# A fused linear-attention and GLU kernel: a shorter warm-up of TensorE, the up weights on another queue, and new orders of all engines

## The chip, the cores and the metric

The kernel runs on one core of one Trainium2 chip. The core has five engines with a queue of instructions each, strictly in order: TensorE (PE in the profile; its weight loads are shown apart as PEld), VectorE (DVE), ScalarE (ACT), GpSimd (POOL) and SyncE (SP, which here only starts DMAs). PE multiplies a stationary tile of weights with a moving tile and writes to PSUM, which has eight banks here; VectorE and ScalarE read PSUM and write SBUF. DMAs started from SP and from ACT stand in two queues, q1 and q10 in the profile. The metric is the time of one execution on the device in microseconds (us); less is better.

## The reference

One transformer block on 2048 rows of 448 columns in bf16: a linear attention with 16 heads of 28 columns, then a gated feed-forward part of width 1792, each with a layer norm ahead and a residual addition behind.

```python
def _A_ref(x, wqkv, wo):
    ...
    phi = lambda t: jnp.where(t > 0, t + 1, jnp.exp(t)) + 1e-6
    pq, pk = phi(q), phi(k)
    kv = jnp.einsum("bhsd,bhse->bhde", pk, v)
    z = jnp.einsum("bhsd->bhd", pk)
    num = jnp.einsum("bhqd,bhde->bhqe", pq, kv)
    den = jnp.einsum("bhqd,bhd->bhq", pq, z)[..., None] + 1e-6
    o = num / den
    ...
def _B_ref(x, w_gate, w_up, w_down):
    ...
    h = _gelu(g) * u
    ...
h = x + _A_ref(_layernorm(x, axis=-1), A_wqkv, A_wo)
h2 = h + _B_ref(_layernorm(h, axis=-1), B_w_gate, B_w_up, B_w_down)
```

## The kernel before

The rows are cut into 16 tiles of 128 (t = 0 to 15). The work has four stages that run into each other.

**Norm and K.** For each tile VectorE takes the statistics (`ln_stats`, L438 and L439), ScalarE turns the variance into rs by a logarithm and an exponential (L445, L447), and the normalized tile xnn is written by VectorE for tiles 0 to 2 (L478) and by GpSimd for the others (L481; from tile 4 on L505, and L508 for the last 64 columns of odd tiles). The PE transposes tiles 0 to 3 (L493), whose results ScalarE (L500) and VectorE (L502) copy into xnT, a part of the tensor hh; from tile 4 on SP starts DMA transposes instead (L512), for single tiles 4 to 7 and for pairs from 8 on. Then PE multiplies with the K weights (`proj1` L534 for tiles 0 and 1, `proj2` L553 for pairs). ScalarE takes the exponential e (L570), VectorE clips it (L571) and makes pk of it (L573), and PE sums the products of pk with the normalized rows over all tiles (`pt_pair`, L588). A group of L553 cannot write its banks before pk of the group that used them is done.

**Q and the small matrices.** The Q products (L553 as well) go to eq and pq (L596, L597). The sums of L588 are copied out, multiplied with the V weights (L629, kv), masked (L633) and multiplied with the output weights (L645, w2).

**Attention output.** For each pair of tiles the denominators are formed by a product with z (L680, GpSimd), a sum (L684) and a reciprocal (L687); pq is scaled (L689, L694), transposed (by PE for the first pair, by DMA L717 later), multiplied with w2 (L734, L749), added to x (L756), and normalized again into hn and its transpose hnT.

**Feed-forward.** `gu_chunk` multiplies gate and up weights with hnT (L872, L874), ScalarE takes the gelu (L896), VectorE the product hm (L898), and PE multiplies with the down weights (L823, L841). The first chunks of 2 tiles stand between the attention output of later pairs.

**What sets the order.** `_Graph.add` records each task with the buffers that it reads and writes. The numbers in ORDERS are those tasks, one string of them per engine: PE, ACT, DVE, POOL, SP. `place` puts them in that order and `plan` works out the semaphore waits that are left. HOLD sets which of several waits of a task comes first. So each engine's queue is written out by hand, and a task that waits holds all behind it.

**Around the change.** The first task of PE is the warm-up `warm_fn` (L422 to L427): WARM matmuls of ones_bf with itself into a bank that nobody reads, as soon as GpSimd has written the ones. The transposes of tile 0 follow, then the task `fill_0`, eight matmuls of the same kind (L433), then K of tile 0. The loads of x and of the Q and K weights are listed in LOADS (L255): SP starts x of tile 0, the K and Q weights and x of tiles 4 to 15, ACT starts x of tiles 1 to 3. The gate and up weights (L614, L615; 1568 KB each, gate to partitions 0 to 63 and up to 64 to 127) are started by SP behind the last DMA transpose of x; behind them in SP's queue stand the copies of w2 (L663) and the transposes of L717. Two memsets of VectorE (L411 on wv_sb, L412 on pt_sb) and some of GpSimd (L397 eps_d, L404 a part of xnn, L410 pqn) and its two selects (L406, L408) prepare buffers and stand wherever ORDERS puts them.

## Time and profile before

| what | before |
|---|---|
| median of 3 runs | 193.06 us (192.75 to 193.07) |
| the profiled execution | 193.89 us |
| its span in the trace | 191.7 us |
| instructions in the trace | 4775, of them 2030 matmuls |
| bytes moved | 17.59 MB |

The profile is one further execution with the hardware profiler on. Its span runs from the first to the last instruction; 2.2 us lie around it. A row of the timeline has the start and the length in us, the engine, the source line, the operation, the tensor written and those read, shapes and count; in square brackets stands the idle time of the engine ahead of it and what ended it. In the rows by stretch, each engine has its busy time and the number of its instructions in the stretch; the last three columns are the recorded clock, the busy share of the DMA engines and GB/s. Matmuls are pipelined: the time of one in a row is longer than the distance to the next. Rows that end in KB and a number are DMA issues: size, and the time from issue to landing.

### The profile page before, as it was taken

Reading aid. Unit: us, or ns where it says so; the run is one execution under the profiler, and the core shown is the slowest. Engines: PE = TensorE matmul, PEld = TensorE weight load, DVE = VectorE, ACT = ScalarE, POOL = GpSimd, SP = SyncE. Lnnn points to the kernel's source line nnn. Section 1 sums busy time; section 2 is a strip of 40 time slices with the busy share of each in tenths; the row PEclk is TensorE's granted clock in tenths of the full one; section 3 lists DMA queues with packets and bytes.
Section 4 is the critical chain, followed back from the end, with each engine's and each line's share of the span. In section 5 each row is a group of like instructions: output and inputs, shape, how many; then the busy total and the mean of one; then the engine's idle time right before and its main releaser. Section 6 shows DMA issues by size and latency. Waiting matters only on the chain.

```text
span 191.7 us, 4775 instructions
## 1 busy us (share of the span) xinstructions
PE 185.4 (97%) x2030; PEld 104.1 (54%) x2030; DVE 124.7 (65%) x260; ACT 71.7 (37%) x164; POOL 53.9 (28%) x102
## 2 busy tenths in 40 slices
PE   7999989999799999999999999999999999999994
PEld 7735545554498758774444444444555444454443
DVE  2699957799999989996858773416444153434222
ACT  3498433678874202322222322121444032442100
POOL 3079930075056538641019003510000000000000
DMA  6924579997649543392050650007400002000004
GB/s 180 336 72 100 115 166 248 208 215 161 98 117 226 140 77 81 72 148 55 13 99 5 144 96 3 0 0 108 87 0 3 0 3 96 0 3 0 0 27 168
DMA packets 34244, 17.59 MB, mean 92 GB/s; under 512 B 27312, under 2 KB 32944, under 8 KB 34224
## 3 DMA queue, kind: packets, MB, share of 16 engines
q1 hardware_dynamic: 33936, 16.95, 40.2%
q8 instruction: 16, 0.26, 0.6%
q10 hardware_dynamic: 288, 0.34, 0.5%
q14 instruction: 4, 0.03, 0.1%
HBM read 8.37 MB, written 1.84 MB: 53 GB/s over the span
## 4 chain that ended last, share of the span: by engine, by line
PE 84%; DVE 4%; POOL 4%; ACT 3%; DMA 2%; issue 1%; POOLq 0%
PE ps L872 42%; PE ps L823 19%; PE ps L553 5%; PE ps L749 5%; PE ps L588 4%; PE ps L425 3%; PE ps L841 3%; DMA hh<-xnn 2%; PE ps L874 2%; POOL xnn L505 2%; DVE st L438 1%; ACT pq L597 1%; POOL xnn L508 1%; ACT ln L445 1%; DVE x_sb L756 1%
## 5 line engine op out<-in xcount | busy, mean ns | idle before, releaser
L872 PE MATMUL ps<-hnT,wgu_sb 64*128 64x512 bf16 (+1 forms) x490 | 88.4, 333 | 0.1
L874 PE MATMUL ps<-hnT,wgu_sb 64*128 64x512 bf16 (+1 forms) x490 | 88.4, 333 | 0.0
L896 ACT ACTIVATE gl<-ps 128x256 bf16<-128x256 f32 (+1 forms) x84 | 34.9, 453 | 87.3 <-PE ps L872 87.3
L898 DVE TENSOR_TENSOR hh<-ps,gl 128x256 bf16<-128x256 f32 (+1 forms) x84 | 40.2, 507 | 40.8 <-ACT gl L896 40.7
L872 PEld LDWEIGHTS ps<-hnT,wgu_sb 64*128 64x128 bf16 x490 | 46.0, 94 | 35.3 <-ACT gl L896 0.5
L874 PEld LDWEIGHTS ps<-hnT,wgu_sb 64*128 64x128 bf16 x490 | 45.9, 94 | 0.5
L823 PE MATMUL ps<-wd_sb,hh 64*128 64x448 bf16 x392 | 39.4, 349 | 0.0
L823 PEld LDWEIGHTS ps<-wd_sb,hh 64*128 64x128 bf16 x392 | 18.9, 94 | 18.6 <-issue 0.4
L680 POOL TENSOR_TENSOR t<-pq,zbc 128x448 f32<-128x448 bf16 x15 | 16.7, 1128 | 30.4 <-DVE zbc L617 12.6
L553 PE MATMUL ps<-wqk_sb,hh 64*128 64x448 bf16 x196 | 23.4, 350 | 1.3 <-DMA hh<-xnn 0.7
L438 DVE BATCH_NORM_STATS2 st<-x_sb 128x6 f32<-128x448 bf16 x32 | 19.0, 609 | 3.5 <-DMA x_sb<-in_A_x_dram 3.4
L588 PE MATMUL ps<-pk,xnn 64*128 64x448 bf16 x128 | 15.5, 349 | 0.4 <-DVE pk L573 0.4
L553 PEld LDWEIGHTS ps<-wqk_sb,hh 64*128 64x128 bf16 x196 | 9.3, 95 | 10.9 <-DMA hh<-xnn 1.1
L828 DVE TENSOR_TENSOR x_sb<-ps,x_sb 128x896 bf16<-128x896 f32 x7 | 7.6, 1090 | 6.5 <-PE ps L823 6.5
L570 ACT ACTIVATE e<-ps 128x896 bf16<-128x896 f32 (+1 forms) x10 | 7.6, 766 | 7.8 <-PE ps L553 7.7
L772 POOL TENSOR_SCALAR hn<-x_sb,nm,rs 128x448 bf16<-128x448 bf16 x14 | 10.1, 727 | 0.5
L749 PE MATMUL ps<-w2p,pqnT 64*128 64x448 bf16 x84 | 9.9, 349 | 0.0
L588 PEld LDWEIGHTS ps<-pk,xnn 64*128 64x128 bf16 x128 | 6.5, 94 | 6.3 <-DVE pk L573 1.1
L756 DVE TENSOR_TENSOR x_sb<-ps,x_sb 128x896 bf16<-128x896 f32 (+1 forms) x9 | 8.7, 973 | 0.6 <-PE ps L749 0.6
L573 DVE SCALAR_TENSOR_TENSOR pk<-ps,e 128x896 bf16<-128x896 f32 (+1 forms) x10 | 8.8, 893 | 0.1
L684 DVE TENSOR_REDUCE den<-t 128x32 f32<-128x896 f32 (+1 forms) x9 | 8.7, 969 | 0.2 <-POOL t L680 0.2
L505 POOL TENSOR_SCALAR xnn<-x_sb,nm,rs 128x448 bf16<-128x448 bf16 (+1 forms) x12 | 8.3, 696 | 0.9 <-ACT rs L447 0.9
(85 smaller groups left out, 141.8 us busy)
## 6 DMA issues: line engine op xcount, KB each, us to landing
wgu_sb<-in_B_w_gate_dram SPq DMA_DIRECT2D x1, 1568.0 KB, 11.4
wgu_sb<-in_B_w_up_dram SPq DMA_DIRECT2D x1, 1568.0 KB, 18.5
out_dram<-x_sb SPq DMA_DIRECT2D x7, 224.0 KB, 2.2
x_sb<-in_A_x_dram SPq DMA_DIRECT2D x3, 448.0 KB, 6.4
wd_sb<-in_B_w_down_dram SPq DMA_DIRECT2D x2, 448.0 KB, 3.9
wqk_sb<-in_A_wqkv_dram SPq DMA_DIRECT2D x2, 336.0 KB, 4.7
wd_sb<-in_B_w_down_dram SPq DMA_DIRECT2D x2, 336.0 KB, 4.1
wo_sb<-in_A_wo_dram SPq DMA_DIRECT2D x1, 392.0 KB, 4.6
```

Source lines behind the costliest of these rows:

```text
L438: op("dve", lambda e: e.bn_stats(st[:, t, :], src_ap), [b_src], [b_st[t]], "bnst%s_%d" % (tag, t))
L505: op("pool", lambda e: e.tensor_scalar(xnn[:, p, o:o + w1], x_sb[:, t, 0:w1], nm1[:, t:t + 1], rs1[:, t:t + 1], ALU.add, ALU.mult), [b_x[t ...
L553: ins = e.matmul(ps[:, bk0 + i_, 0:D], xnT[HALF[h], t, c, :], wqk_sb[HALF[h], c, c0:c0 + D], start=(part == "a" and c == 0), stop=(c == 3))
L588: ins = e.matmul(ps[:, BK_PT[c], 0:D], xnn[HALF[h], t // 2, tcols(t, c)], pk[HALF[h], t % PK_R, :], start=(t == 0 and o == 0), stop=(t == ...
L680: op(eng, lambda e, t=t, n=n: e.tensor_tensor(t1[:, n, :], pq[:, t, :], zbc[:, :], ALU.mult), [b_pq[t]] + b_z, [b_t1[n]], "t1%s_%d" % (eng ...
L749: ins = e.matmul(ps[:, BK_OUT[n], 0:D], pqnT[rows, i2, n, g, :], w[rows, g, :], start=(g == 0 and s == 0), stop=(g == 3 and s == 1))
L756: op("dve", lambda e, t=t, bo=bo, m=m: e.tensor_tensor(x_sb[:, t:t + m, :], ps[:, bo:bo + m, 0:D], x_sb[:, t:t + m, :], ALU.add), b_ps[bo: ...
L823: ins = e.matmul(ps[:, BK_O[n], 0:D], hh[HALF[h], j, (t % HR) * 128:(t % HR + 1) * 128], wd_sb[HALF[h], j, :], start=(s == 0 and j == 0), ...
L872: first = e.matmul(psG[:, jj * N:(jj + 1) * N], wgu_sb[A_, k, j * 128:(j + 1) * 128], hnT[A_, r0:r0 + nt, ka_, :], start=(k == 0), stop=(k ...
L874: ins = e.matmul(psU[:, jj * N:(jj + 1) * N], wgu_sb[B_, k, j * 128:(j + 1) * 128], hnT[B_, r0:r0 + nt, kb_, :], start=(k == 0), stop=(k = ...
L896: G.add("act", lambda e, gi=gi, cs_=cs_, psG=psG: e.activation(gl[:, gi, cs_], psG[:, cs_], AF.Gelu_apprx_tanh), r=[b_ps[BK_G[i]]], w=b_gl ...
L898: op("dve", lambda e, dst=dst, srcU=srcU, srcL=srcL: e.tensor_tensor(dst, srcU, srcL, ALU.mult), [b_ps[bu]] + b_glh, [b_ar[j_][t % HR] for ...
```

## The change

WARM becomes 58, and each warm-up matmul writes 64 columns where it wrote 128. The eight of the fill stay as they are. The up weights are started by ScalarE's queue and not by SyncE's. ORDERS and HOLD are new for all five engines. The line of WARM_N is added, so each line behind it has a number one higher in the changed kernel.

```diff
 ORDERS = (
...
-    "1 3 26 30 31 38 39 34 46 47 62 54 42 55 66 67 50 98 99 59 69 105 106 81 122 82 123 85 129 130 148 149 94 95 168"
...
+    "1 3 26 30 31 38 34 39 46 47 62 42 54 55 67 50 66 98 99 59 69 105 106 122 82 81 123 85 129 130 148 149 95 94 168"
...
-    WARM = 56
+    WARM = 58
+    WARM_N = 64
...
         def warm_fn(e):
             ins = None
             for _ in range(WARM):
-                ins = e.matmul(ps[:, 3, 0:128], ones_bf[:], ones_bf[:], start=True, stop=True)
+                ins = e.matmul(ps[:, 3, 0:WARM_N], ones_bf[:], ones_bf[:, 0:WARM_N], start=True, stop=True)
             return ins
...
         dma("sp", wgu_sb[A_, :, :], B_w_gate.rearrange("(k p) n -> p k n", p=64), b_wg, "dwg0", behind=xts[-1:])
-        dma("sp", wgu_sb[B_, :, :], B_w_up.rearrange("(k p) n -> p k n", p=64), b_wu, "dwu0", behind=xts[-1:])
+        dma("act", wgu_sb[B_, :, :], B_w_up.rearrange("(k p) n -> p k n", p=64), b_wu, "dwu0", behind=xts[-1:])
```

`dma` turns `behind` into a place in the same queue if the transpose was started by the same engine, and into a wait for its landing if not. So ScalarE now waits for the last DMA transpose of x, at a place between the exponential of tiles 12 and 13 and those of tiles 15 and 14; SyncE's queue has the copies of w2 right behind gate.

The orders at three places. First the start of VectorE's queue. BN_STATS and BN_AGGR are the statistics of a tile, TENSOR_SCALAR on xnn is a normalization (the first that of tile 0), and COPY takes the transposes of a tile out of PSUM. Before:

```order
L438 BN_STATS st1<-x_sb 128x6
L439 BN_AGGR mv1<-st1 128x2
L438 BN_STATS st1<-x_sb 128x6
L411 MEMSET wv_sb 64x224
L478 TENSOR_SCALAR xnn<-x_sb,mv1,rs1 128x448
L439 BN_AGGR mv1<-st1 128x2
L438 BN_STATS st1<-x_sb 128x6
L502 COPY hh<-ps 128x4x64
```

After:

```order
L439 BN_STATS st1<-x_sb 128x6
L440 BN_AGGR mv1<-st1 128x2
L439 BN_STATS st1<-x_sb 128x6
L479 TENSOR_SCALAR xnn<-x_sb,mv1,rs1 128x448
L440 BN_AGGR mv1<-st1 128x2
L439 BN_STATS st1<-x_sb 128x6
L503 COPY hh<-ps 128x4x64
```

The memset of wv_sb has left the place ahead of the first normalization.

Second, VectorE around the clip and pk of tiles 4 and 5 and, further on, of tiles 12 and 13. The 128x896 rows on e1 are clips of a pair, SCALAR_TENSOR_TENSOR is pk of a pair, and the rows on eq and pq prepare Q. Before:

```order
L438 BN_STATS st1<-x_sb 128x6 x2
L439 BN_AGGR mv1<-st1 128x2 x2
L571 TENSOR_SCALAR e1<-e1 128x896
L573 SCALAR_TENSOR_TENSOR pk<-ps,e1 128x896
...
L571 TENSOR_SCALAR e1<-e1 128x896
L573 SCALAR_TENSOR_TENSOR pk<-ps,e1 128x896
L571 TENSOR_SCALAR e1<-e1 128x448 x2
```

After:

```order
L439 BN_STATS st1<-x_sb 128x6 x3
L440 BN_AGGR mv1<-st1 128x2 x2
L572 TENSOR_SCALAR e1<-e1 128x896
L574 SCALAR_TENSOR_TENSOR pk<-ps,e1 128x896
...
L572 TENSOR_SCALAR e1<-e1 128x896
L412 MEMSET wv_sb 64x224
L574 SCALAR_TENSOR_TENSOR pk<-ps,e1 128x896
```

Three statistics in a row, not two, stand ahead of the clip of tiles 4 and 5, and the memset of wv_sb now stands between clip and pk of tiles 12 and 13.

Third, GpSimd from tile 7 to the pair of tiles 10 and 11, whose DMA transpose starts when both are normalized. The rows on nm1 negate means, the rows of 128x448, 128x384 and 128x64 on xnn are normalizations. Before:

```order
L505 TENSOR_SCALAR xnn<-x_sb,nm1,rs1 128x384
L508 TENSOR_SCALAR xnn<-x_sb,nm1,rs1 128x64
L442 TENSOR_SCALAR nm1<-mv1 128x2
L508 TENSOR_SCALAR xnn<-x_sb,nm1,rs1 128x64
L505 TENSOR_SCALAR xnn<-x_sb,nm1,rs1 128x448
L408 AFFINE_SELECT mask<-mtmp 112x4
L505 TENSOR_SCALAR xnn<-x_sb,nm1,rs1 128x384
L442 TENSOR_SCALAR nm1<-mv1 128x2
L508 TENSOR_SCALAR xnn<-x_sb,nm1,rs1 128x64
L505 TENSOR_SCALAR xnn<-x_sb,nm1,rs1 128x384
L397 MEMSET eps_d 128x1
L442 TENSOR_SCALAR nm1<-mv1 128x2
```

After:

```order
L443 TENSOR_SCALAR nm1<-mv1 128x2
L398 MEMSET eps_d 128x1
L509 TENSOR_SCALAR xnn<-x_sb,nm1,rs1 128x64
L506 TENSOR_SCALAR xnn<-x_sb,nm1,rs1 128x384
L509 TENSOR_SCALAR xnn<-x_sb,nm1,rs1 128x64
L506 TENSOR_SCALAR xnn<-x_sb,nm1,rs1 128x448
L443 TENSOR_SCALAR nm1<-mv1 128x2
L411 MEMSET pqn 128x16x16
L506 TENSOR_SCALAR xnn<-x_sb,nm1,rs1 128x448
L509 TENSOR_SCALAR xnn<-x_sb,nm1,rs1 128x64
L405 MEMSET xnn 128x6x64
L506 TENSOR_SCALAR xnn<-x_sb,nm1,rs1 128x384
```

The memsets of pqn and of a part of xnn, which stood ahead of tile 4, now stand between the normalizations of tiles 10 and 11, and the select L408 has moved behind the last normalization.

On PE the groups of L588 change places with the K products of later tiles (pt of tiles 2 and 3 stands one group later), the w2 products stand together ahead of Q of tiles 10 and 11, both parts of the output product of tiles 4 and 5 stand together, and most gate and up groups run in rising order where before each second pair was swapped.

72 rows, old and new, of tables (HOLD, ORDERS) are left out of this document.

## The prediction

> **What bounds the kernel now.** I read the page first, then the busy time by stage, then the timeline of TensorE (PE) where a stage shows idle time, and last the timelines of the engine that PE waits for there.
>
> The page, its span and the busy time of each engine:
>
> ```profile
> span 191.7 us, 4775 instructions
> PE 185.4 (97%) x2030; PEld 104.1 (54%) x2030; DVE 124.7 (65%) x260; ACT 71.7 (37%) x164; POOL 53.9 (28%) x102
> ```
>
> PE is the bound, but a share of the span doesn't say where it waits. Busy time by stage, columns as the heading of the view has them (stretch, its length, busy time of each engine):
>
> ```profile
> 25.65:40.20 14.55, 14.55 (x153) 7.30 (x153) 10.75 (x20) 6.73 (x11) 1.99 (x3) 1.00 0.97 218
> 40.20:61.70 21.50, 20.28 (x293) 14.17 (x292) 20.23 (x41) 16.55 (x30) 9.86 (x12) 1.00 0.74 151
> 61.70:190.00 128.30, 127.49 (x1352) 68.13 (x1352) 74.12 (x148) 32.78 (x83) 25.84 (x46) 1.00 0.26 53
> ```
>
> From 61.70 us on PE is busy 127.49 of 128.30 us, and the change leaves it the same 1352 matmuls. So nothing can be won there; the new orders can only lose. From 25.65 to 40.20 PE has no idle time at all: when that stretch starts sets when the rest ends. What can be won lies ahead of 25.65, and up to 1.2 us between 40.20 and 61.70. PE's timeline ahead of 25.65 (start, length, line, count, idle time before it):
>
> ```profile
> 1.05 5.95 PE L425 MATMUL ps<-ones_bf 128*128 128x128 bf16 x56 [1.05 <-POOL eps_t L396]
> 6.93 0.29 PE L493 MATMUL ps<-ident,xnn 64*128 64x64 bf16 x8
> 7.15 0.62 PE L433 MATMUL ps<-ones_bf 128*128 128x128 bf16 x8
> 7.70 1.03 PE L534 MATMUL ps<-wqk_sb,hh 128*128 128x448 bf16 x4
> 8.78 1.03 PE L534 MATMUL ps<-wqk_sb,hh 128*128 128x448 bf16 x4
> 12.42 0.72 PE L553 MATMUL ps<-wqk_sb,hh 64*128 64x448 bf16 x5 [0.43 <-ACT hh L500]
> 21.60 0.93 PE L588 MATMUL ps<-pk,xnn 64*128 64x448 bf16 x8 [0.41 <-DVE pk L573]
> 25.65 0.74 PE L553 MATMUL ps<-wqk_sb,hh 64*128 64x448 bf16 x6 [0.66 <-DMA hh<-xnn]
> ```
>
> The 56 warm-up matmuls hold the transposes of tile 0 (L493) until 6.93. After them PE waits three times: for an evacuation on ScalarE (0.43), for pk on VectorE (0.41), and for a DMA transpose (0.66).
>
> **The warm-up.** Its pace is the only place where the trace shows PE's clock, since the clock column says 1.00 throughout. Matmuls of L425 by stretch:
>
> ```profile
> 1.00:3.20 2.20, 2.15 (x21) 2.15 (x22) 1.00 0.60 124
> 3.20:6.60 3.40, 3.40 (x35) 3.40 (x34) 1.00 1.11 337
> 6.92 0.17 PEld L493 LDWEIGHTS ps<-ident,xnn 64*128 64x128 bf16 x8
> ```
>
> The 56 take 5.95 us, one per 0.106, and up to 6.60 the stretches keep that pace (35 are in flight in 3.40 us, some three of them begun before). The eight fills of L433 right after take 0.62 us in all, under 0.08 each with the last one's drain. So PE runs at half pace until about 6.6 us and at full pace from there. At half pace 64 columns should take half of 0.106; the weight loads are no hindrance, since eight loads of 128 columns took 0.17 us at full pace (0.021 each, 0.04 at half pace). Estimate: 58 x 0.053 = 3.1 us, and the warm-up ends at 4.15 instead of 7.00.
>
> Who then comes last? VectorE and ScalarE ahead of tile 0, and the loads (size, us from issue to landing):
>
> ```profile
> 4.60 0.20 ACT L447 ACTIVATE rs<-ln 128x1 f32<-128x1 f32 x1
> 4.86 0.24 DVE L411 MEMSET wv_sb<- 64x224 uint32 x1
> 5.13 0.40 DVE L478 TENSOR_SCALAR xnn<-x_sb,mv,rs 128x448 bf16<-128x448 bf16 x1
> 1.25 1.02 SPq L359 DMA_DIRECT2D wqk_sb<-in_A_wqkv_dram  x2
> wqk_sb<-in_A_wqkv_dram SPq DMA_DIRECT2D x1, 112.0 KB, 4.4
> 3.48 0.58 SPq L359 DMA_DIRECT2D x_sb<-in_A_x_dram  x1
> x_sb<-in_A_x_dram SPq DMA_DIRECT2D x1, 448.0 KB, 5.9
> ```
>
> The memset of wv_sb leaves its place ahead of tile 0's normalization (L478), which then starts at 4.84 behind rs (4.80) and ends at 5.24, not 5.53. Transposes start at about 5.3, the fills follow (eight at half pace, 0.86 us, to 6.35), and the K weights land at 1.7 + 4.4 = 6.1. K of tile 0 starts at about 6.4 instead of 7.70: 1.3 us earlier, if PE runs at full pace.
>
> Here I have to choose. Before, PE was busy without a break for 5.5 us (1.05 to 6.6) when the pace doubled. Now it is busy for 3.1, idle for 1.1 and busy again from 5.3. I take it that the break starts the count anew, so that the pace doubles by 5.3 + 5.5 = 10.8 at the latest, and reckon with 10.4. [...]
>
> At half pace the four matmuls of 448 columns take 4 x 0.374 = 1.5 us and eight transposes some 0.3, so a step from one projection to the next is 1.8 instead of the 1.08 between 7.70 and 8.78. K of tile 1 starts at 6.4 + 2 x 1.8 = 10.0, and before it was 7.70 + 2 x 1.08 = 9.87. So the lead of 1.3 us is gone by then. What is left: ScalarE and VectorE have done more of tiles 0 and 1 by then, the second memset (L412, same kind) no longer sits ahead of the first pk, and the row at 12.42, which waited for ScalarE, comes at about 12.1: **-0.3** (between -0.7, half the lead, and +0.2).
>
> **Pair by pair to 25.65.** VectorE around the wait at 21.60, then the piece of the chain of work that ended last from 21.20 on, and the times to landing of the transposes of x:
>
> ```profile
> 18.44 0.61 DVE L438 BATCH_NORM_STATS2 st<-x_sb 128x6 f32<-128x448 bf16 x1
> 19.67 0.75 DVE L571 TENSOR_SCALAR e<-e 128x896 bf16<-128x896 bf16 x1 [0.34 <-ACT e L570]
> 20.45 1.09 DVE L573 SCALAR_TENSOR_TENSOR pk<-ps,e 128x896 bf16<-128x896 f32 x1
> 21.20 4.40 DMA hh<-xnn
> DMA to landing us min/median/max: 2.4/2.8/4.4
> ```
>
> Three statistics now stand ahead of this e (L571), not two: 0.61 less the 0.34 of idle time is +0.27 on pk, so of the 0.3 only **-0.03** is left at 21.60. PE was done at 24.99 (25.65 less 0.66) and would now be at 24.96. The transpose of tiles 10 and 11 ended 4.40 us after GpSimd was done at 21.20, against a median of 2.8. GpSimd:
>
> ```profile
> 12.10 0.71 POOL L505 TENSOR_SCALAR xnn<-x_sb,nm,rs 128x448 bf16<-128x448 bf16 x1 [0.36 <-ACT rs L447]
> 10.62 0.31 POOL L410 MEMSET pqn<- 128x256 bf16 x1
> 10.87 0.42 POOL L404 MEMSET xnn<- 128x384 bf16 x1
> 18.02 0.19 POOL L408 TENSOR_SCALAR_AFFINE_SELECT mask<-mtmp 112x4 f32<-112x4 f32 x1
> q8 instruction: 1, 0.02, 5.0%
> ```
>
> Two memsets (0.73 us) move from idle time into the dense run between tile 4 and tile 11, one select (0.19) leaves it: 21.2 - 12.1 = 9.1 becomes 9.2 to 9.6, since up to 0.4 of waits in it can absorb some. With tile 4 at 11.8 (0.3 earlier, as its transposes on PE are) the last is done at about 21.1, and the transpose lands at 23.9 (median) or 25.5 (as slow as before). A 16 KB instruction load ran between 23.2 and 24.6 (last row), beside the slow one's end; it follows PE's progress, which hardly moves against the transpose, so neither case can be left out. K of tiles 10 and 11 starts at 24.96 or at 25.5: -0.69 or -0.15, and I take the middle, **-0.42**.
>
> **Later.** The memset of wv_sb now stands between an e and its pk (tiles 12 and 13), the pk that Q of tiles 4 and 5 waits for:
>
> ```profile
> 31.79 1.09 DVE L573 SCALAR_TENSOR_TENSOR pk<-ps,e 128x896 bf16<-128x896 f32 x1
> 33.04 0.73 PE L553 MATMUL ps<-wqk_sb,hh 64*128 64x448 bf16 x6
> ```
>
> pk ended at 32.88, PE started at 33.04 without a wait and could not have by 0.1 us more: 0.24 of memset and 0.1 of gaps less 0.1 is **+0.24** (0 to +0.35).
>
> The up weights on ScalarE's queue, the gate and up rows of the same view:
>
> ```profile
> wgu_sb<-in_B_w_gate_dram SPq DMA_DIRECT2D x1, 1568.0 KB, 11.4
> wgu_sb<-in_B_w_up_dram SPq DMA_DIRECT2D x1, 1568.0 KB, 18.5
> 29.06 0.62 SPq L359 DMA_DIRECT2D wgu_sb<-in_B_w_up_dram  x1
> 32.87 0.98 ACT L570 ACTIVATE e<-ps 128x448 bf16<-128x448 f32 x2 [1.54 <-PE ps L553]
> 52.49 0.27 PE L872 MATMUL ps<-hnT,wgu_sb 64*128 64x256 bf16 x1
> ```
>
> They landed at 29.1 + 18.5 = 47.6, and their first use is at 52.49, so 4.9 us of cover remain whether they come sooner or, beside gate, as late as now. The issue, some 0.6 us on ScalarE, waits there for the last transpose of x with the e of tiles 14 and 15 queued behind; that e idled 1.54 us for a product of the same transpose. Zero, and +0.3 if that transpose lands late.
>
> From 40.20 to 61.70 the regrouped w2, Q and output products fill waits that sit beside a latency chain of VectorE and ScalarE, which stays: **-0.07** for the small ones that go (-0.3 to +0.5; the upper end is the product hm of L898 ahead of the first down projection, behind two copies and an addition now).
>
> **Sum:** -0.42 + 0.24 - 0.07 = -0.25 us (the -0.3 and -0.03 are contained in -0.42). The profiled execution took 193.89 us, 2.2 of it outside its span; it would take 193.64. The median of the runs shown is 193.06, 0.83 below the profiled one, and the difference carries over: 192.8.
>
> **Rivals.** *The pace doubles at about 6.65 all the same.* Then the lead of 1.3 us is kept, 1.4 with the memset; tile 4 is bound by its load, 3.48 + 5.9 = 9.4, which leaves GpSimd about 1.4 as well. At 21.60 -1.13 is left. PE is done at 23.86, the transpose lands at 22.9 to 24.5: K of tiles 10 and 11 at 23.86 to 24.5, -1.79 to -1.15, middle -1.47; with the later terms -1.3, so 191.8. For it: 1.1 us of idle time is short. Against: 5.5 busy microseconds were needed before.
>
> *The pace comes later still,* because the projections at half pace leave small gaps and the count starts only with the closer work from about 8 us on: 8.0 + 5.5 = 13.5. K of tile 1, the transposes of tile 3 and Q of tile 1 run at half pace too; the row at 12.42 comes at about 13.4, +1.0, and that at 21.60 at +1.2. PE is done at 26.2, after any transpose: +0.5; with +0.24 and -0.07 it is +0.7, so 193.8. It decides from a doubling at about 11.3 us on; before that the idle time at 25.65 absorbs it. For it: the gaps of the projections are in the rows of before (a step of 1.08 us holds four matmuls of 0.2 and eight transposes). Against: the break of 1.1 us is far longer than those.
>
> *The small matmuls are no shorter,* because each loads 128 columns of weights, and the warm-up ends near 7 as now. Then only the moved statistics, memsets and selects count: GpSimd is done near 21.4, PE is done at 25.26 (+0.27), the transpose lands at 24.2 to 25.8: -0.39 to +0.15, with the later terms about zero, 193.1. The row of the weight loads speaks against it. [...]
>
> **How the numbers follow.** Forecast 0.48, early pace 0.28, late pace 0.16, no shorter 0.08. About 0.2%, 0.39 us, is what a measurement of this kernel can tell from no change. The forecast's own range is 192.3 to 193.4; its middle lies inside no change but near its edge, so it gives 0.18 to faster, 0.25 to same, 0.05 to slower. Early pace is faster but for 0.01 of same; late pace gives 0.11 to slower and 0.05 to same; the last gives 0.06 to same and 0.01 to each side. Together 0.46, 0.37, 0.17. The range, 191.5 to 193.6, leaves out some 0.18: the lower third of early pace and over half of late pace.
>
> **What would show it.** L425's rows, now L426: 58 in about 3.1 us. The first K row near 6.4, with a step to the next of 1.8 (forecast), 1.1 (early pace). The row at 12.42 near 12.1, that at 25.65 between 24.9 and 25.5, Q at 33.04 with a wait for pk of about 0.2. The prediction is wrong if the first step is 1.1, or if PE shows idle time past 61.7, where the new order would have cost what the front won.

## The result and the profile after

| what | before | after |
|---|---|---|
| median of the runs of the comparison | 193.06 us (192.75 to 193.81, 4 runs) | 195.92 us (193.56 to 196.18, 4 runs) |
| ratio, 95% interval | | 1.012 (1.0074 to 1.0166) |
| profiled execution, its span | 193.89 us, 191.7 us | 196.02 us, 194.3 us |
| timed again on a second chip, 12 runs | 193.34 | 193.80 (192.40 to 195.44), ratio 1.0024 (0.9996 to 1.0053) |
| timed again on a third chip, 12 runs | 192.84 | 194.48 (192.75 to 196.19), ratio 1.0057 (1.0035 to 1.0080) |

The change makes the kernel slower, in two of the three comparisons by more than the noise, and it spreads its times: over the three comparisons its 28 runs go from 192.40 to 196.19, while 127 runs of the kernel before in the later comparisons lie between 192.46 and 194.41. Seven of the 28 have a mean clock of 0.99; before has 0.999 or more in all. A ratio leaves out runs over 1.5% above the fastest of their kernel, most of which have the lower clock, so the medians, which are over all runs, say more here.

The page of the changed kernel: its span, the busy time of PE, and the two rows of 40 slices for PE and its clock.

```profile
span 194.3 us, 4777 instructions
PE 186.6 (96%) x2032; PEld 102.5 (53%) x2032; DVE 124.9 (64%) x260; ACT 71.7 (37%) x164; POOL 53.8 (28%) x102
PE   6999959999989999999999999999999999999995
PEclk9999978999999999999999999999999999999999
```

A slice is 4.86 us: PE is idle for almost half of the sixth (from 24.3 us), and its clock is lower in the sixth and the seventh. PE's timeline, first the front, then from 21 us on:

```profile
1.05 3.27 PE L426 MATMUL ps<-ones_bf 128*128 128x64 bf16 x58 [1.05 <-POOL eps_t L397]
5.29 0.40 PE L494 MATMUL ps<-ident,xnn 64*128 64x64 bf16 x8 [0.97 <-DVE xnn L479]
6.52 1.76 PE L535 MATMUL ps<-wqk_sb,hh 128*128 128x448 bf16 x4
8.43 1.67 PE L535 MATMUL ps<-wqk_sb,hh 128*128 128x448 bf16 x4
10.15 1.03 PE L535 MATMUL ps<-wqk_sb,hh 128*128 128x448 bf16 x4
...
21.14 0.93 PE L589 MATMUL ps<-pk,xnn 64*128 64x448 bf16 x8
23.61 0.92 PE L589 MATMUL ps<-pk,xnn 64*128 64x448 bf16 x8
26.52 0.94 PE L554 MATMUL ps<-wqk_sb,hh 64*128 64x448 bf16 x6 [2.00 <-DMA hh<-xnn]
28.01 1.70 PE L554 MATMUL ps<-wqk_sb,hh 64*128 64x448 bf16 x8
29.50 1.71 PE L589 MATMUL ps<-pk,xnn 64*128 64x448 bf16 x12
31.05 0.73 PE L554 MATMUL ps<-wqk_sb,hh 64*128 64x448 bf16 x6
```

The front is close to the forecast: a warm-up of 3.27 us with its last matmul's end, K of tile 0 at half pace at 6.52, K of tile 1 at 10.15 at full pace. The row of 21.60 is now at 21.14 and waits for nothing. Then K of tiles 10 and 11 starts at 26.52 instead of 25.65, behind 2.00 us of idle time, and from 27 to 30.3 us the groups take twice as long. The row that stood at 28.50 stands at 31.05: +2.55 us, where the spans differ by 2.6. Its row in the kernel before:

```profile
28.50 0.73 PE L553 MATMUL ps<-wqk_sb,hh 64*128 64x448 bf16 x6
```

The chain of work that ended last has the transpose it waits for as one piece of 5.23 us (4.40 before), and the DMA queues in the middle of it, from 23.0 to 24.6 us, hold two loads of instructions (q8 is the 16 KB block of the prediction's last GpSimd row):

```profile
21.24 5.23 DMA hh<-xnn
...
q8 instruction: 1, 0.02, 5.6%
q14 instruction: 1, 0.01, 5.5%
```

The trace's record of TensorE's clock changes at 9.86, 26.93 and 30.34 us; the distances are 17.07 and 3.41, that is 5 and 1 times 3.413. Busy time by stretch, cut at those edges:

```profile
20.11:23.52 3.41, 3.41 (x38) 1.67 (x36) 3.04 (x6) 1.44 (x4) 3.31 (x8) 1.00 0.67 138
23.52:26.93 3.41, 1.42 (x18) 0.52 (x14) 2.19 (x4) 0.92 (x1) 2.12 (x5) 1.00 0.90 91
26.93:30.34 3.41, 3.41 (x22) 1.39 (x20) 0.00 (x0) 0.59 (x1) 0.00 (x0) 0.50 1.05 256
64.50:192.60 128.10, 127.50 (x1352) 68.31 (x1352) 74.51 (x148) 33.11 (x83) 26.27 (x46) 1.00 0.26 53
```

In the stretch in which PE waits it is busy for 1.42 of 3.41 us, and for the whole next stretch its clock is 0.50: 22 matmuls where 38 to 40 fit, some 1.7 us. From 64.5 us on nothing is lost.

### The profile page after: what moved, and what is told of

The parts are those of the page before. It is cut to its first block, busy times and chain, and to the rows that moved or that the text cites. A ratio compares the mean times of both kernels' runs of the same rounds, so it can differ in the third digit from the quotient of the medians.

```text
span 194.3 us, 4777 instructions
## 1 busy us (share of the span) xinstructions
PE 186.6 (96%) x2032; PEld 102.5 (53%) x2032; DVE 124.9 (64%) x260; ACT 71.7 (37%) x164; POOL 53.8 (28%) x102
## 4 chain that ended last, share of the span: by engine, by line
PE 81%; DMA 6%; DVE 5%; POOL 4%; ACT 3%; issue 1%; POOLq 0%
PE ps L873 42%; PE ps L824 19%; PE ps L750 5%; PE ps L554 4%; PE ps L589 3%; PE ps L842 3%; DMA hh<-xnn 3%; DMA pqnT<-pqn 2%; POOL xnn L506 2%; PE ps L875 2%; PE ps L535 1%; DMA x_sb<-in_A_x_dram 1%; DVE pqn L690 1%; POOL xnn L509 1%; ACT e L571 1%
## 5 line engine op out<-in xcount | busy, mean ns | idle before, releaser
L554 PE MATMUL ps<-wqk_sb,hh 64*128 64x448 bf16 x196 | 24.5, 362 | 2.2 <-DMA hh<-xnn 2.0
L681 POOL TENSOR_TENSOR t<-pq,zbc 128x448 f32<-128x448 bf16 x15 | 17.6, 1182 | 31.5 <-DVE zbc L618 15.4
L589 PE MATMUL ps<-pk,xnn 64*128 64x448 bf16 x128 | 16.5, 364 | 0.0
L554 PEld LDWEIGHTS ps<-wqk_sb,hh 64*128 64x128 bf16 x196 | 9.4, 96 | 12.7 <-DMA hh<-xnn 2.4
## 6 DMA issues: line engine op xcount, KB each, us to landing
wgu_sb<-in_B_w_gate_dram SPq DMA_DIRECT2D x1, 1568.0 KB, 12.3
```

The source lines that it names most:

```text
L554: ins = e.matmul(ps[:, bk0 + i_, 0:D], xnT[HALF[h], t, c, :], wqk_sb[HALF[h], c, c0:c0 + D], start=(part == "a" and c == 0), stop=(c == 3))
L589: ins = e.matmul(ps[:, BK_PT[c], 0:D], xnn[HALF[h], t // 2, tcols(t, c)], pk[HALF[h], t % PK_R, :], start=(t == 0 and o == 0), stop=(t == ...
L681: op(eng, lambda e, t=t, n=n: e.tensor_tensor(t1[:, n, :], pq[:, t, :], zbc[:, :], ALU.mult), [b_pq[t]] + b_z, [b_t1[n]], "t1%s_%d" % (eng ...
```

## The experiments

Theory at the start: PE's wait of 2 us for the transpose of tiles 10 and 11, and the fall of the clock behind it, are the loss. Rivals: the short warm-up as such (A), GpSimd's order that starts the transpose late (B), another cause of the fall (C). What came out is a fourth: two things that the prediction took as fixed, the phase of the clock (where in an execution the edges lie at which it changes; it first opens at 9.86 us in after, at 3.85 in e5 and 3.82 in f1) and the place of an instruction load among the transposes (23.41 us in before, 23.07 in after), decide together. In the table a fall is a run with a mean clock of 0.99 or less. A clock that opens late does not show in this figure, since the record of the clock begins with the first opening (in after at 9.86 us, though the K row at 6.52 is at half pace). The last column has the pair of tiles whose K products (a K row, L554) PE waited for longest in the one profiled execution, and this idle time:

| run | median, range (runs) | before beside it | ratio (95%) | falls | K row, idle |
|---|---|---|---|---|---|
| e1_warm_only | 193.47, 192.46 to 193.82 (12) | 193.39 | 1.000 (0.998 to 1.002) | 0 | 10/11, 0.50 |
| e2_long_warm | 193.61, 192.77 to 195.60 (12) | 193.39 | 1.0019 (0.9994 to 1.0045) | 1 | 10/11, 1.23 |
| e3_pool_front | 193.27, 192.01 to 193.79 (12) | 193.39 | 0.9992 (0.9970 to 1.0015) | 0 | 10/11, 0.75 |
| e4_gap_fill | 194.30, 193.10 to 195.54 (12) | 193.39 | 1.0049 (1.0024 to 1.0074) | 1 | none |
| e5_after_again | 193.80, 192.40 to 195.44 (12) | 193.34 | 1.0024 (0.9996 to 1.0053) | 0 | 10/11, 1.53 |
| e6_fewer_instr | 193.66, 192.28 to 194.98 (12) | 193.34 | 1.0024 (0.9996 to 1.0052) | 0 | 12/13, 0.40 |
| e7_real_fill | 193.28, 191.74 to 195.21 (10) | 193.34 | 0.9991 (0.9970 to 1.0013) | 1 | 10/11, 0.35 |
| e8_up_on_sp | 192.75 (1) | 193.34 | | 0 | 10/11, 1.55 |
| e9_warm80 | 191.63, 191.02 to 192.47 (6) | 193.17 | 0.9921 (0.9897 to 0.9945) | 0 | 10/11, 0.44 |
| e10_best80 | 194.04, 192.84 to 195.34 (12) | 193.17 | 1.0037 (1.0006 to 1.0068) | 6 | 8/9, 2.20 |
| e11_best40 | 192.00, 191.40 to 192.19 (6) | 193.17 | 0.9934 (0.9917 to 0.9951) | 0 | 14/15, 0.45 |
| e12_longer_wait | 194.30, 193.01 to 195.02 (10) | 193.17 | 1.0041 (1.0017 to 1.0065) | 1 | 10/11, 1.65 |
| f1_after_third | 194.48, 192.75 to 196.19 (12) | 192.84 | 1.0057 (1.0035 to 1.0080) | 4 | 10/11, 1.10 |
| f2_warm58x88 | 192.96, 192.62 to 193.35 (12) | 192.84 | 0.9994 (0.9977 to 1.0011) | 0 | 10/11, 1.72 |
| f3_warm80_wv | 191.83, 191.27 to 195.22 (7) | 192.84 | 0.9923 (0.9901 to 0.9946) | 2 | 8/9, 2.09 |
| f4_before_warm80 | 193.84, 193.16 to 195.61 (12) | 192.84 | 1.0059 (1.0034 to 1.0084) | 2 | 8/9, 1.77 |
| g1_warm40_wv | 192.30, 191.97 to 192.43 (6) | 193.17 | 0.9947 (0.9927 to 0.9968) | 0 | 12/13, 0.26 |
| g2_best40_again | 191.61, 191.26 to 192.00 (6) | 193.17 | 0.9912 (0.9890 to 0.9934) | 0 | 4/5, 0.30 |

### Which part of the change

**e1**, the warm-up alone, in the kernel before:

```diff
-    WARM = 56
+    WARM = 58
+    WARM_N = 64
-                ins = e.matmul(ps[:, 3, 0:128], ones_bf[:], ones_bf[:], start=True, stop=True)
+                ins = e.matmul(ps[:, 3, 0:WARM_N], ones_bf[:], ones_bf[:, 0:WARM_N], start=True, stop=True)
```

> The kernel before with one part of the change: 58 warm-up matmuls of 64 columns. Orders and queues are those of before. Theory (the late DMA transpose of tiles 10 and 11 lets PE idle for 2 us, and the clock then falls to half for 3.4 us): the warm-up alone moves K of tile 0 forward by 1.2 us but GpSimd's order, and with it the start of that transpose, stays; the row at 25.65 comes between 25.2 and 25.7, no fall of the clock, 192.7 to 193.1. Rival A (the short warm-up itself leaves the clock gate in another phase, so that the next short idle closes it): the fall of the clock is here too, clock 0.99 and 195 to 196.

**e2**, everything but the warm-up:

```diff
-    WARM = 58
-    WARM_N = 64
+    WARM = 56
+    WARM_N = 128
```

> The changed kernel with the old warm-up, 56 matmuls of 128 columns; orders and queues stay as changed. Rival A (the warm-up): no fall of the clock, no idle time above 1 us before K of tiles 10 and 11, 193.2 to 193.6 (the 0.24 of the memset of wv_sb stays). Rival B (the orders: the memsets among GpSimd's normalizations put the transpose late): K of tiles 10 and 11 at 26 or later, the clock falls, 195 to 196.

**e3**, GpSimd's first 40 tasks in the order of before (first line shown):

```diff
-    "10 12 16 17 18 11 56 57 20 100 101 107 108 109 124 131 125 21 132 150 13 133 152 153 151 170 23 171 173 19 172"
+    "10 12 17 16 11 20 18 56 57 23 19 100 101 107 108 109 124 131 125 21 132 133 150 153 151 22 152 170 173 172 13"
```

> The changed kernel with GpSimd's order of before up to tile 15's normalization: the memsets of pqn and of xnn stand ahead of tile 4 again. Rival B: the transpose of tiles 10 and 11 starts 0.5 to 0.7 us earlier, at about 20.6, and lands near 23.5, so K of tiles 10 and 11 starts at about 24.6, the clock does not fall, and the time is 192.3 to 192.8. If the landing is set by something else (an instruction load that holds one DMA ring), the wait stays near 2 us and the time at 195 to 196.

**e8**, the up weights back on SyncE, their task (259) in SyncE's order behind 258:

```diff
-        dma("act", wgu_sb[B_, :, :], B_w_up.rearrange("(k p) n -> p k n", p=64), b_wu, "dwu0", behind=xts[-1:])
+        dma("sp", wgu_sb[B_, :, :], B_w_up.rearrange("(k p) n -> p k n", p=64), b_wu, "dwu0", behind=xts[-1:])
```

> The changed kernel with the up weights back on SyncE's queue, right behind the gate weights. Step 6 of the prediction: the up weights land at 47 to 49 either way and no row waits for them, so this makes no difference to the rows of PE from 40 to 62 us. Rival (the issue on ScalarE delays an exponential, or the two loads beside each other delay those of wd or the transposes of pq): the rows of PE from 33 to 62 us come 0.2 us or more earlier against their start at 33 than in the changed kernel.

The warm-up alone shows no effect in 12 runs (e1), so A falls as the sole cause; nor does any run show that the warm-up sets the phase, since three executions of the changed kernel open the clock at 9.86, 3.85 and 3.82 us. Everything else without it gives 0.19% with an interval that holds zero and one fall in 12 (e2). GpSimd's old order has a median 0.5 us below e5's, but on another chip, with overlapping intervals and without a fall in either (e3): a share of B is possible and not shown, and the transpose still sets K of tiles 10 and 11. Both parts together make 0.24 (an interval that holds zero as well) and 0.57% in e5 and f1; whether they add or need each other these intervals don't tell. The queue of the up weights costs nothing: from kv (39.66 us) to the end of the span e8 takes 151.3 us, the changed kernel 151.3 (42.99 to 194.3).

### The clock

**e5** and **f1** are the changed kernel, unaltered.

> The changed kernel once more, unaltered, so that its times can be set beside those of its variants on one chip, and a second trace of it. If the clock falls only where the idle time before K of tiles 10 and 11 is about 2 us, as in the first trace, the runs split into some near 193.5 with a clock of 1.00 and some near 196 with 0.99, and a trace with a clock of 1.00 shows that idle time at 1.6 us or less. Rival (the clock falls whatever the idle time): a trace of either kind with idle times that do not fit.

> The changed kernel a third time, unaltered. If both times so far are draws from one spread (clock open at 4 to 5 or at 8.4 to 10.6, and a fall of the clock where the idle time ahead of K of tiles 10 and 11 fills more than about 55% of one window): 192.4 to 194.4 for runs with a clock of 1.00, 195.4 to 196.2 for those with 0.99, and some of each. If the falls of the first comparison were something of that chip alone: none again, median 193.6 to 194.0.

The front of e5's trace on PE:

```profile
1.05 3.11 PE L426 MATMUL ps<-ones_bf 128*128 128x64 bf16 x58 [1.05 <-POOL eps_t L397]
5.28 0.29 PE L494 MATMUL ps<-ident,xnn 64*128 64x64 bf16 x8 [1.11 <-DVE xnn L479]
6.16 1.02 PE L535 MATMUL ps<-wqk_sb,hh 128*128 128x448 bf16 x4
8.31 1.03 PE L535 MATMUL ps<-wqk_sb,hh 128*128 128x448 bf16 x4
```

The same instructions as in the first trace, but PE is at full pace from 3.85 us on, and K of tile 1 starts at 8.31, not at 10.15. In f1's trace the clock opens at 3.82, falls at 7.24 and opens again at 10.65. Two stretches of e5, then three of f1:

```profile
0.44:3.85 3.41, 2.80 (x53) 2.81 (x54) 0.47 (x1) 1.28 (x1) 1.55 (x8) 1.00 0.49 142
20.92:24.33 3.41, 1.98 (x22) 0.80 (x18) 2.35 (x4) 0.95 (x2) 3.09 (x7) 1.00 0.82 134
```

```profile
0.41:3.82 3.41, 2.77 (x53) 2.77 (x54) 0.49 (x1) 1.28 (x1) 1.58 (x9) 1.00 0.52 134
3.82:7.24 3.42, 1.52 (x28) 1.06 (x26) 2.62 (x9) 1.57 (x7) 0.00 (x0) 1.00 1.09 312
7.24:10.65 3.41, 3.41 (x25) 1.30 (x23) 2.09 (x8) 1.68 (x6) 1.01 (x3) 0.50 0.98 362
```

So the first opening lies elsewhere in each execution: at 3.85 (e5), 3.82 (f1), 9.86 (after) and, in other traces of kernels with the short warm-up, at 3.90 (e3), 4.46 (e8), 4.92 (e4), 5.05 (e12) and 9.39 (e6); further edges are 3.413 us or a multiple of it away. What opens it is estimated from PE's busy time in the 3.413 us ahead of an edge: 2.69 us (e12, 1.64 to 5.05) or more opened the clock (2.77 in f1, 2.80 in e5, 3.27 in e8); 2.62 (e9, 0.26 to 3.67), 2.50 (e6, 2.56 to 5.97) and 2.45 (after, 3.03 to 6.45) did not. Open, it stayed open over 1.76 (e12, 22.12 to 25.53) and 1.98 (e5, 20.92 to 24.33), and fell over 1.52 (f1, 3.82 to 7.24) and less (1.42 in after, 1.21 in e10). With the idle time behind the short warm-up (0.97 us in after, 1.06 in f1, 1.11 in e5) the clock stayed shut until 9.86 in after and shut again at 7.24 in f1 (there with 0.83 us more ahead of K of tile 0), and in e5 it was open from 3.85 on.

**e4**, 11 matmuls of no use in the wait (the task stands ahead of K of tiles 10 and 11 in PE's order):

```diff
+                    for i in range(GAP_FILL):
+                        ins = e.matmul(ps[:, bk0 + i % 2, 0:D], ones_bf[:], wqk_sb[:, 0, 0:D], start=True, stop=True)
```

> The changed kernel with 11 matmuls of 448 columns, whose results nobody reads, ahead of K of tiles 10 and 11, in the two banks that this group overwrites: 2.0 us of work in the idle time. Theory (idle time makes the clock fall): K of tiles 10 and 11 still starts near 26.5, but the clock stays at 1.00 and the rows from 26.5 on keep the pace of 0.19 per pair: 193.8 to 194.4, in every run. Rival C (the clock falls for another reason, the load of work after the wait or a power limit): still 0.99 and 195.5 to 196.5.

**e12**, a longer wait:

```diff
-        op("pool", lambda e: e.memset(pqn[:, :, :, :, GW:128], 0.0), [], [b for l in b_pqn for b in l], "pqnpad")
+        def pqnpad_fn(e):
+            e.memset(idle_sb[:], 0.0)
+            return e.memset(pqn[:, :, :, :, GW:128], 0.0)
+        op("pool", pqnpad_fn, [], [b for l in b_pqn for b in l], "pqnpad")
```

> The changed kernel with one more memset of GpSimd, of 1024 elements in a scratch buffer, ahead of that of pqn: the normalization of tile 11 and its transpose come about 0.9 us later, and PE idles for 2.5 to 3 us ahead of K of tiles 10 and 11. Theory (a window in which PE idles for more than about 55% halves the clock for the next): a fall of the clock in most runs, with 0.99 and 196 to 197, the others near 194.7. Rival (the fall in the first trace had nothing to do with the idle time): a clock of 1.00 in nearly all runs, 194.4 to 195.

Its 55%, as that of f1's expectation, is an estimate between e5, whose stretch of 3.41 us with 1.43 of idle time (42%) kept the clock open, and after, where 1.99 (58%) shut it; e12's own 1.65 (48%) and f1's 1.90 (56%) narrow it.

Both are inconclusive. e4 kept PE busy in the gap, but one run of 12 has a clock of 0.99 all the same (194.47; by f1's trace that can be a fall in the front), and its median is not lower; in its trace the 11 matmuls also hold K of tiles 10 and 11 until 25.64, though the transpose had landed at 25.01. e12 did not lengthen the wait: PE itself was held by a GpSimd memset at 20.11 for 0.37 us, the idle time came out at 1.65, and one run of 10 fell.

### The load of instructions

Each of these DMA transposes ends in the traces with 16 reports to its semaphore; a report is taken here for that of one ring (DMA queue), and the last for the landing, since K starts behind it (in before the last comes at 25.61 us, K of tiles 10 and 11 at 25.65). In the trace of before, 15 of the 16 rings of this transpose report by 23.97 us and the last at 25.61, while a 16 KB load takes 1.12 us from 23.41, 2.2 us after the transpose's issue. In e1, e2, e3 and f1 it is the same: the load begins 2.1 to 2.2 us after the issue, 15 rings are early, one is 1.5 to 1.7 us late, and the transpose takes 4.2 to 4.5 us. In after, e4, e5, e7, e8 and f2 the load begins 1.8 to 2.05 us after the issue, and then all 16 rings report late: 4.8 to 5.2 us.

The DMA packets of the traces say more. Each of these transposes ends with 32 packets of 4 bytes. In all eleven traces 30 of them begin 2.08 to 2.27 us after the issue and two at 3.1 to 4.0 us, so by these packets one ring is late either way. What differs is whether the load begins behind the first of these packets (2.08 us), and then 15 rings report on time, or ahead of it, and then all rings report late (in after from 25.97 to 26.48, behind the late packets at 25.25). In f3 and f4, too, the load begins just ahead of such packets, 2.2 and 2.3 us after the issue of the transpose of tiles 8 and 9 and the packets at 2.34, and all rings report late. In e12 and e9 the load is over before these packets (it begins 0.5 and 0.9 us after the issue); they come about 1 us late, and the transpose takes 4.5 and 3.7 us.

**e6** moves the load:

```diff
-    WARM = 58
-    WARM_N = 64
+    WARM = 29
+    WARM_N = 128
```

> The changed kernel with 29 warm-up matmuls of 128 columns instead of 58 of 64: the same 3.1 us with 29 matmuls and 29 weight loads fewer. Theory (the load of 16 KB of TensorE's instructions, which in each trace so far begins at 22.0 to 23.4, holds one of the 16 DMA rings while the transpose of tiles 10 and 11 moves its data, and this ring sets when K of tiles 10 and 11 starts): the load comes 29 matmuls later in the program, behind the start of K of tiles 10 and 11; the transpose lands at 23.5 to 24.0 on all rings, this K starts as soon as PE is free, at 24.5 to 24.8, the clock stays at 1.00 in all runs, 192.1 to 192.7. Rival B (the transpose is late because GpSimd finishes late): no change, K at 25.5 or later, 193.5 to 196.

PE from 24.8 us on, and the load's row from 26.1 to 27.2:

```profile
24.85 0.73 PE L554 MATMUL ps<-wqk_sb,hh 64*128 64x448 bf16 x6
26.55 1.30 PE L589 MATMUL ps<-pk,xnn 64*128 64x448 bf16 x12
28.25 0.74 PE L554 MATMUL ps<-wqk_sb,hh 64*128 64x448 bf16 x6 [0.40 <-DMA hh<-xnn]
...
q8 instruction: 1, 0.02, 5.5%
```

The wait at tiles 10 and 11 is gone (24.85, against 26.52), their transpose takes 2.85 us, and with the load the late ring has moved to tiles 12 and 13 (15 rings by 26.70, the last at 28.21). The time is not better: this front has idle time too (0.91 us), and in its trace the clock opens only at 9.39. **e9** closes that gap with 80 small matmuls (`WARM = 80`), **e10** adds e3's order and moves the memset of wv_sb (24) ahead of the clip of tiles 10 and 11 (178):

```diff
-    " 164 167 165 186 206 184 187 185 114 115 204 205 207 138 139 158 159 276 178 179 315 198 24 199 277 316 221 222"
+    " 164 167 165 186 206 184 187 185 114 115 204 205 207 138 139 158 159 276 24 178 179 315 198 199 277 316 221 222"
-    WARM = 58
+    WARM = 80
```

> The changed kernel with 80 warm-up matmuls of 64 columns: 4.2 us instead of 3.1, so that the warm-up ends at about 5.3, when the transposes of tile 0 can start, and not 1.1 us ahead of them. Theory (the clock is judged in windows of 3.41 us that run on by themselves, begin anywhere in an execution, and open the clock only if PE was busy for about 80% of one): with 58 matmuls the window that the idle time falls into fails, so in some executions the pace doubles at 4 to 5 us and in others only at 8.4 to 10.6; with 80 no window from 1.05 us on fails and the pace doubles by 7.3 at the latest. The slow end of the runs moves in: median 192.8 to 193.4, highest without a later fall of the clock below 194.0. Rival (what decides is the late transpose of tiles 10 and 11, whatever the front does): median 193.7 to 193.9 as in the changed kernel.

> 80 warm-up matmuls of 64 columns, GpSimd's order of before up to tile 15's normalization, and the memset of wv_sb ahead of the clip of tiles 10 and 11, where VectorE has 1.6 us of idle time. If the three terms add: the front 0.5, the transpose of tiles 10 and 11 0.5 earlier, Q of tiles 4 and 5 0.24 earlier: median 192.0 to 192.6, faster than the kernel before by 0.4 to 0.7%. If an instruction load holds a ring of that transpose whatever is done: 192.8 to 193.3.

The 3.41 us in e9's expectation are the distance of the edges above, and its 80% is an estimate between 2.80 us of 3.413 (82%, opened) and 2.50 (73%, did not); e12's 2.69 (79%) and e9's 2.62 (77%) narrow it. e9 gained more than expected. e10 was to be faster still and is slower than before. PE in e10, and its busy time around the wait:

```profile
20.14 0.93 PE L589 MATMUL ps<-pk,xnn 64*128 64x448 bf16 x8
23.28 0.74 PE L554 MATMUL ps<-wqk_sb,hh 64*128 64x448 bf16 x6 [2.20 <-DMA hh<-xnn]
24.23 1.52 PE L554 MATMUL ps<-wqk_sb,hh 64*128 64x448 bf16 x8
25.54 1.70 PE L589 MATMUL ps<-pk,xnn 64*128 64x448 bf16 x8
```

```profile
21.01:24.42 3.41, 1.21 (x14) 0.60 (x14) 1.84 (x2) 0.50 (x3) 3.06 (x7) 1.00 1.06 134
24.42:27.83 3.41, 3.41 (x22) 1.44 (x20) 1.05 (x2) 0.92 (x1) 0.00 (x0) 0.50 1.06 220
```

The load now comes at 19.58 us, into the transpose of tiles 8 and 9; K of these waits 2.20 us, PE is busy for 1.21 us of that stretch of 3.41, and the clock is at half for the next. Six of 12 runs fell. **f4** puts the 80 small matmuls into the kernel before, with the same end, a load at 19.99 and K of tiles 8 and 9 behind 1.77 us:

```diff
-    WARM = 56
+    WARM = 80
+    WARM_N = 64
```

> The kernel before with 80 warm-up matmuls of 64 columns, 4.2 us instead of 5.95; orders and queues of before. If the front alone makes the gain of the changed kernel with 80: 191.7 to 192.3. If the new orders are needed (before waits 0.41 for pk of tiles 4 and 5 at 21.60 and GpSimd ends its part at the same time whatever the front does): 192.6 to 193.2.

**f2** separates the two causes: no idle time behind the warm-up, but the instruction count of the change.

```diff
-    WARM_N = 64
+    WARM_N = 88
```

> The changed kernel with 58 warm-up matmuls of 88 columns: 4.2 us without idle time behind them as with 80 of 64, but with the number of instructions of the changed kernel, so the 16 KB load comes where it came there. Theory of the idle time (most of the 2.2 us between 58 and 80 small matmuls is the clock that opens late): 191.6 to 192.4. Rival (most of it is the place of the load, which hits the transpose of tiles 10 and 11 here): 192.8 to 193.6, K of tiles 10 and 11 behind an idle time of 1.2 us or more.

f2 lies between: 192.96 beside 194.48 for the changed kernel on the same chip, with a spread of 0.7 us instead of 3.4 and no fall. So closing the front's gap is worth some 1.5 us there, and the place of the load the rest, about 1.3 us to e9 (another chip; 0.9994 against 0.9921 of before). Neither theory had all of it, and the two do not simply add: e6 moves the load and leaves the gap, and gains nothing. In f2's trace the wait at tiles 10 and 11 is there:

```profile
1.05 4.44 PE L426 MATMUL ps<-ones_bf 128*128 128x88 bf16 x58 [1.05 <-POOL eps_t L397]
24.82 0.74 PE L554 MATMUL ps<-wqk_sb,hh 64*128 64x448 bf16 x6 [1.72 <-DMA hh<-xnn]
```

### Versions

**e7** puts real work into the wait: pt products of tiles 6 and 7 (140, 141, 143) ahead of K of tiles 10 and 11 (175).

```diff
-    " 156 117 142 175 140 176 141 143 160 195 162 196 163 215 161 216 180 182 231 181 232 200 183 201 223 224 202 225"
+    " 156 117 142 140 141 143 175 176 160 195 162 196 163 215 161 216 180 182 231 181 232 200 183 201 223 224 202 225"
```

> The changed kernel with the pt products pt31, pt30 and pt10 of tiles 6 and 7 (12 matmuls, some 1.1 us) moved ahead of K of tiles 10 and 11 in PE's order. Theory: the transpose lands as late as before the move, but PE works for 1.1 us of the wait, so that at most 1.0 us of it is idle; the clock stays at 1.00 and of the 1.1 us most comes back: 192.4 to 193.2. Rival (the chain behind K of tiles 10 and 11, the exponential, the clip and pk, is what the next groups wait for): the rows from 28 us on wait for pk, and it is 193.5 or more.

Its median is 0.5 us below that of the change (193.28 beside 193.80, overlapping intervals) and level with the kernel before. **f3** is e9 with the memset moved as in e10; **e11** and **g2** are e10 with 40 matmuls of 128 columns; **g1** is the same with GpSimd's order as changed.

```diff
-    WARM = 58
-    WARM_N = 64
+    WARM = 40
+    WARM_N = 128
```

> The changed kernel with 80 small matmuls, and the memset of wv_sb ahead of the clip of tiles 10 and 11, where VectorE idles 1.6 us. Step 5 of the prediction (0.24 for Q of tiles 4 and 5): 0.2 to 0.3 below the kernel with 80 small matmuls alone (191.63), so 191.3 to 191.5, and the idle time of 0.24 ahead of Q of tiles 4 and 5 gone. Rival (the work behind it is bound by VectorE anyway): the same 191.6.

> As the kernel with 80 small matmuls, GpSimd's old front and the moved memset, but the warm-up as 40 matmuls of 128 columns: the same 4.2 us with 40 matmuls and weight loads fewer, so the 16 KB load of TensorE's instructions comes some 3.5 us later in the program. Theory (the ring with that load sets the landing): K of tiles 10 and 11 starts without a wait for its transpose, and if a transpose is hit it is that of tiles 12 and 13 or 14 and 15, whose K has about 1.5 us of slack: 191.8 to 192.4, 0.2 to 0.5 below the other. Rival (the landing follows GpSimd alone): the two are the same within 0.2.

> The changed kernel with 40 warm-up matmuls of 128 columns (4.2 us, 40 matmuls fewer than with 80 small ones) and the memset of wv_sb ahead of the clip of tiles 10 and 11; GpSimd's order stays as changed. Theory: no idle time behind the warm-up, so the clock opens by 7.3; the load of instructions comes at 23 to 24.5, behind most of the transpose of tiles 10 and 11, so no row of K waits over 1 us and no run shows a fall of the clock: 191.4 to 192.2. Rival (GpSimd's order puts that transpose 0.5 us later, so that the load still catches its last ring): K of tiles 10 and 11 behind 1.2 us or more, 192.4 to 193.4.

> The kernel with 40 matmuls of 128 columns, GpSimd's order of before up to tile 15's normalization and the moved memset once more, on another chip: 191.4 to 192.3 and a clock of 1.00 throughout if its first result (192.0, six runs) was no luck; a run of 194 or more with 0.99 would show that the load still meets a transpose in some executions.

g2's PE rows, the warm-up, K of tiles 10 and 11 and of 12 and 13, and Q of tiles 4 and 5 with the row ahead:

```profile
1.05 4.04 PE L426 MATMUL ps<-ones_bf 128*128 128x128 bf16 x40 [1.05 <-POOL eps_t L397]
23.98 0.73 PE L554 MATMUL ps<-wqk_sb,hh 64*128 64x448 bf16 x6
27.21 0.74 PE L554 MATMUL ps<-wqk_sb,hh 64*128 64x448 bf16 x6 [0.23 <-DMA hh<-xnn]
31.00 0.92 PE L589 MATMUL ps<-pk,xnn 64*128 64x448 bf16 x8
31.76 0.73 PE L554 MATMUL ps<-wqk_sb,hh 64*128 64x448 bf16 x6
```

With the load at 23.88 us the transpose of tiles 10 and 11 takes 2.8 us, and no K row waits over 0.30. The clearest test of the load's place is e10 beside e11: on one chip, with the same orders and the same number of warm-up columns, 80 matmuls of 64 columns give 194.04 and six falls, 40 of 128 columns 192.00 and none. g2 is the fastest version that held on two chips: 191.61 and 192.00, ratios 0.9912 (0.989 to 0.9934) and 0.9934 (0.9917 to 0.9951), with no fall. GpSimd's old order is worth 0.7 us beside g1 on the same chip. f3 shows the risk of e9's place: in its trace the load comes at 19.33, tiles 8 and 9 wait 2.09 us, and two of seven runs fell, to 194.41 and 195.22. In e9's trace, with the same instructions of PE, the load came 2 us later (21.36) and the transpose of tiles 8 and 9 had landed (20.90), so the good result of e9's six runs may be luck.

## Why the prediction was wrong

**The warm-up**: right for the first trace within 0.2 us in its rows, the warm-up, K at 6.52, steps of 1.9 and 1.7 us and the row of 12.42 at 12.3; the full pace came at 9.86 (10.4, at most 10.8). Its 0.021 us is not the time of a weight load: the eight loads of that row overlap, and one takes 0.09 us (L493 in before). The conclusion held, 58 matmuls with their loads took 3.1 to 3.3 us. It failed in taking the moment of the opening as a property of the kernel. It reckoned with a count of 5.5 busy microseconds that a break starts anew, and 10.4 was a choice within that; no run shows such a count: in e5 the clock opened at 3.85 behind 2.80 us of work. The edges lie elsewhere in each execution, so the forecast's pace and the rival *the pace doubles at about 6.65 all the same* are both true, in different executions of the same code: e5's trace is the rival's (K of tile 1 at 8.31, 192.40 us against its 191.8).

**Pair by pair to 25.65** is the step that failed. "K of tiles 10 and 11 starts at 24.96 or at 25.5" became 26.52, 24.43 and 25.93 in the three traces of the change, behind 2.00, 1.53 and 1.10 us of idle time. The forecast had PE wait 0.54 us there at most. GpSimd was done at 21.22, against 21.1. The row of 21.60 came 0.46 earlier, not 0.03, because the clip behind the three statistics took 0.36 us where before's row at 19.67 has 0.75; VectorE in after:

```profile
19.59 0.36 DVE L572 TENSOR_SCALAR e<-e 128x896 bf16<-128x896 bf16 x1
```

What failed is "it follows PE's progress, which hardly moves against the transpose": with PE 0.46 ahead the load came 0.35 us earlier (23.07) and the transpose 0.05 later, so it began 1.8 us after the issue and not 2.2, ahead of the transpose's last packets, and all rings reported late. The gain of PE ended in a longer wait. And this wait was counted as idle time that only ends; that it can halve the clock for 3.41 us was in no rival. In the first trace that is +0.87 for the start and 1.7 for the clock, 2.55 in all, where -0.42 stood.

**The memset of wv_sb**: +0.24, as forecast. From the pt row to Q of tiles 4 and 5 it is 1.00 us in the changed kernel, and 0.76 in g2 (31.00 to 31.76), where the memset is moved:

```profile
34.84 0.92 PE L589 MATMUL ps<-pk,xnn 64*128 64x448 bf16 x8
35.84 0.74 PE L554 MATMUL ps<-wqk_sb,hh 64*128 64x448 bf16 x6
```

Its worth in the total was not resolved: f3 and e9, on two chips, have the same ratio.

**The up weights**: zero, as forecast (e8). **From 40.20 on**: -0.2 rather than -0.07; from kv to the end of the span the changed kernel takes 151.3 us and before 151.5 (40.18 to 191.7). *The small matmuls are no shorter* fell with the first row (58 loads of 128 columns in 3.1 us); *the pace comes later still* named 193.8, near the medians, by another mechanism.

What stays open: no run shows why the reports of the other 15 rings are late too when the load begins ahead of the last packets. The phase of a run without a trace is not known, so that its time belongs to an early or a late opening is argued from the profiled ones.

## What to carry to other kernels

A front that left TensorE idle for some 1.1 us, a third of the 3.41 between edges, traded a sure start for a draw (K of tile 1 at 8.31 us in e5, at 10.15 in after); keep it busy, by filler if need be, until the real work comes, and time the kernel often enough to see the draw. Filler alone is no gain: in the kernel before, the closed front ended in a longer wait (f4, 193.84 beside 192.84). A lead that ends at a wait for a DMA is worth nothing until that DMA's own delays are known (0.46 us earlier at 21.14, and 2.00 of idle time at 26.52), and a long wait cost twice where the clock fell behind it (in after some 1.7 us more). Count instructions too: 36 to 80 of TensorE's more or fewer moved a 16 KB load of them onto or off a transfer that is waited for.

## What the runs showed of the hardware

A 16 KB load of TensorE's instructions is one packet in queue q8 and took 0.9 to 1.6 us; beside it a transpose's last ring reported up to 1.7 us behind the others. 36 to 80 instructions (matmuls and weight loads) more or fewer ahead of it moved the wait from one pair of tiles to another. The trace of after has 16 such loads and 4064 matmuls and weight loads, 254 to a load, which is why they are taken for TensorE's. In 19 of the 20 traces the second of these loads begins when PE has begun 439 to 468 of its matmuls and weight loads, at 19.3 to 26.2 us; in e9's it is 484. PE's longest idle time ahead of a K row was 0.26 us (g1) to 2.20 (e10) in the traces of the variants that have one.

The record of the clock held edges that are multiples of 3.413 us apart in every trace that has them (187.73 us is 55 of them), and the first opening in kernels with the short warm-up lay between 3.82 us (f1) and 9.86 (after). 64-column matmuls ran one per 53 ns at half pace (after), and executions of the same code on one chip differ by up to 4.0 us (f3, 191.27 to 195.22).
